# The first tile of chunk attention feeding a GELU MLP: reciprocals by fp32 transposes, an earlier half of w_in, and the last AV inside mm1

## The chip, the core and the metric

The kernel runs on one core of a Trainium2 chip. The metric is the device time of one execution in microseconds (us); the time before is the median of three runs. A profile of one execution gives a span, from its first to its last instruction, which is about 2 us shorter than the device time.

## What is computed

The reference does attention within chunks of 64 positions (batch 8, 8 heads, 576 positions, head size 64) and feeds the result, as 4608 tokens of 512 features, to a two-layer MLP with the exact GELU between the layers (512 to 2048 to 512). Everything comes in and goes out as float32.

```python
scores = scale * np.matmul(q_c, k_c.transpose(0, 1, 2, 4, 3))      # 9 chunks of 64 x 64 for each head
scores = scores - np.max(scores, axis=-1, keepdims=True)
attn = np.exp(scores)
attn = attn / (np.sum(attn, axis=-1, keepdims=True) + 1e-09)
out = np.matmul(attn, v_c)
x = np.ascontiguousarray(attn_out.transpose(0, 2, 1, 3)).reshape(B * S, H * D)
h = x @ w_in
g = 0.5 * h * (1.0 + erf(h * inv_sqrt2))
return (g @ w_out).astype(np.float32)
```

## The kernel before

**Tiles.** There are nine tiles of 512 tokens. Tiles 0 to 7 are the first eight chunks of one batch entry each; tile 8 gathers the ninth chunk of all eight entries. Heads go in pairs, so a tile has four groups g, each of 128 features (two heads of 64). Matmuls take bf16 operands, cast on the chip from float32 arrivals that lie in six stage buffers.

**Attention of tile 0.** For each group, `att_Tq` and `att_Tk` (L147 and L153) transpose q and k on TensorE and copy them out of PSUM; k goes in two halves into a block-diagonal tile `k_bd`. `att_S` (L187) makes the scores and their exponential `pT`. Then the sums of the exponentials are taken, inverted and spread over the partitions as `rc`. Groups 0 and 1 do that with `att_sum` (L197): a matmul with ones, a 32 x 32 transpose on VectorE, a reciprocal and another transpose. Groups 2 and 3 use `att_sum_pe` (L262): four matmuls of two columns, a reciprocal on VectorE, and, in its inner function `spread`, fp32 matmuls with an identity on TensorE (L276) and a copy on ScalarE. `att_av` (L284) multiplies with V on TensorE (L289) and then makes `x[:, g]` on VectorE as the product of that and `rc` (L296).

**The MLP of a tile** is `phase` (L387). Its first half, mm1, has 16 slots f; each is four matmuls (ks = 0 to 3, L328) that take the four groups of x in turn, then a Gelu on ScalarE (L331). `first` slots are done together, ks by ks, and `between` names functions that are called ahead of a given ks of these. Its second half, mm2 (L384 for tile 0, L344 otherwise), multiplies with w_out. `extra1` and `extra2` name attention work of the next tile that is called between the slots.

**Who sets the order.** Everything stands under a manual schedule: each engine has one queue, and its instructions stand in it in the order in which the Python code emits them. A call of `att_av` therefore places its matmuls in TensorE's queue and its multiply in VectorE's queue at that point of the program. The code emits, in this order: the loads of tile 0's q and k, of V, and of w_in's parts 0 to 2; the attention of tile 0, which ends with `A[3]()`; the load of w_in's part 3 and of w_out, with q and k of tile 1 between; all casts of w_in, of most of w_out and of tile 1's q, k and V, on VectorE, ScalarE and GpSimd (`DV`, `AC`, `PO`); then `phase(0, ...)`, with tile 1's attention inside its second half; then the other tiles. w_in comes in four parts of 512 columns, each cast in four pieces `win[c](i, engine)`; slot f needs piece f % 4 of part f // 4. All loads go through one queue of the sync engine. `keep_warm` issues matmuls that only keep TensorE busy.

Of the kernel before, what the change touches and what calls it, by code (L numbers as in the profile page):

```python
# [11 lines left out]
def kernel(  # L12
# [9 lines left out]
    nc = tc.nc  # L22
    P = 128
    f32 = mybir.dt.float32
# [3 lines left out]
    B, H, S, D = q.shape  # L28
    CH = 64
    NC = S // CH  # L30
    J = 4
    PC = CH // J
    G = H // 2
# [4 lines left out]
    MT = CT * CH  # L38
# [20 lines left out]
    ident_f = consts.tile([P, P], f32, name="ident_f")  # L59
# [9 lines left out]
    k_bds = [consts.tile([P, CT, P], bf16, name=f"k_bd{i}") for i in range(G)]  # L69
# [22 lines left out]
    ps_mm = ctx.enter_context(tc.tile_pool(name="ps_mm", bufs=3, space=bass.MemoryType.PSUM))  # L92
    ps_tp = ctx.enter_context(tc.tile_pool(name="ps_tp", bufs=2, space=bass.MemoryType.PSUM))
# [9 lines left out]
    def load_qk(t, nm, h0=0, h1=H):  # L103

        st = tiles[t]
        src = q if nm == "q" else k
        if nm + "f" not in st:
            st[nm + "f"] = stage_tile()[:].rearrange("p (h j d) -> p h j d", h=H, j=J)
            st[nm] = ld.tile([P, G, J, 2, D], bf16, tag=nm, name=f"{nm}_nat")
        raw = st[nm + "f"]  # L110
        if t < B:
            nc.sync.dma_start(raw[:, h0:h1], src[t, h0:h1, 0:MT, :].rearrange("h (p j) d -> p h j d", j=J))  # L112
        else:
            for b in range(B):
                nc.sync.dma_start(
                    raw[PC * b:PC * (b + 1), h0:h1],
                    src[b, h0:h1, MT:S, :].rearrange("h (p j) d -> p h j d", j=J))

    def load_v(t, gs=range(G)):
        if "vf" not in tiles[t]:  # L120
            tiles[t]["vf"] = stage_tile()[:].rearrange("p (g i d) -> p g i d", g=G, d=D)
        vf = tiles[t]["vf"]
        for g in gs:
            for r in range(2):
                if t < B:
                    src = v[t, 2 * g + r, 0:MT, :].rearrange("(i key) d -> key i d", key=CH)
                else:
                    src = v[:, 2 * g + r, MT:S, :].rearrange("b key d -> key b d")
                nc.sync.dma_start(vf[CH * r:CH * (r + 1), g], src)

    def cast_qk(t, nm, g, copy):
        st = tiles[t]
        copy(st[nm][:, g].rearrange("p j r d -> p r j d"), st[nm + "f"][:, 2 * g:2 * g + 2])  # L133

    def cast_v(t, r, copy, gs=slice(0, G)):
        sl = slice(CH * r, CH * (r + 1))
        copy(v_bds[t % NV][sl, :, gs, sl].rearrange("p i g d -> p g i d"), tiles[t]["vf"][sl, gs])  # L137
# [9 lines left out]
    def att_Tq(t, g, copy):  # L147
        tp = transposed(t, "q", g)
        qT = work.tile([P, CT, CH], bf16, tag="qT", name="qT", bufs=5)
        copy(qT[:].rearrange("p i (c j) -> p i c j", j=J), tp)  # L150
        tiles[t]["qT", g] = qT

    def att_Tk(t, g, copy):  # L153
        tp = transposed(t, "k", g)
        for r in range(2):
            sl = slice(CH * r, CH * (r + 1))
            copy(k_bds[g][sl, :, sl].rearrange("p i (c j) -> p i c j", j=J), tp[sl])  # L157


    def flip(t, nm):  # L160
# [101 lines left out]
    def att_sum_pe(t, g):  # L262

        pT = tiles[t]["pT", g]
        sT = ps_at.tile([P, MT // P, 2], f32, tag="at", name="sT")
        for m in range(MT // P):
            nc.tensor.matmul(sT[:, m], pT[:].rearrange("p i c -> p (i c)")[:, m * P:(m + 1) * P], ones_r[:],
                             start=True, stop=True)
        rr = work.tile([P, MT // P, 2], f32, tag="rr", name="rr", bufs=2)
        nc.vector.reciprocal(rr[:], sT[:])  # L270

        def spread():
            rc_ps = ps_mm.tile([P, MT], f32, tag="mm", name="rc_ps")
            for m in range(MT // P):
                for r in range(2):
                    nc.tensor.matmul(rc_ps[CH * r:CH * (r + 1), m * P:(m + 1) * P],  # L276
                                     rr[:, m, r:r + 1].to_broadcast([P, D]), ident_f[:],
                                     start=True, stop=True, tile_position=(0, CH * r))
            rc = work.tile([P, NB, 32], f32, tag="rc", name="rc", bufs=4)
            nc.scalar.copy(rc[:].rearrange("p n e -> p (n e)"), rc_ps[:])  # L280
            tiles[t]["rc", g] = rc
        return spread

# [14 lines left out]
    NB = MT // 32  # L298
    DV, AC, PO = nc.vector.tensor_copy, nc.scalar.copy, nc.gpsimd.tensor_copy

    def att_units(t, cq=DV, ck=DV):
        tiles[t]["x"] = xpool.tile([P, G, MT], bf16, tag="x", name="x")
        T = []
        for g in range(G):
            T += [lambda g=g: att_Tq(t, g, cq), lambda g=g: att_Tk(t, g, ck if t == 0 or g < 2 else DV)]
        S_ = [lambda g=g: att_S(t, g) for g in range(G)]
        if t > 1:
            T = [lambda g=g: flip_k(t, g, ck) for g in range(G)]
            S_ = [lambda g=g: (att_S_flipped(t, g), att_part(t, g)) for g in range(G)]
        if t > 0:  # L310
            U = [lambda g=g: att_total(t, g, g + 2) for g in (0, 2)] + [lambda g=g: att_rc(t, g) for g in range(G)]
        else:
            U = [lambda g=g: att_sum(t, g) for g in range(G)]
        A = [lambda g=g: att_av(t, g) for g in range(G)]
        return T, S_, U, A
# [71 lines left out]
    def phase(t, extra1, extra2, by_rows=False, between={}):  # L387
        nms = MT // P
        order = [(ms, qt) for ms in range(nms) for qt in range(NQ)]
        if by_rows:  # L390
            order = [(None, f) for f in range(FF - FC)] + [(ms, NQ - 1) for ms in range(nms)]
        first = 3 if t == 1 else 1
        mm1_slot(t, 0, first, between)
        for f in range(first, FF):
            for u in extra1.get(f, ()):
                u()
            mm1_slot(t, f)
        for s, (ms, qt) in enumerate(order):
            for u in extra2.get(s, ()):
                u()  # L400
            if ms is None:
                mm2_rows(t, qt)
            else:
                mm2_slot(t, ms, qt)
        for u in extra2.get("end", ()):
            u()
# [6 lines left out]
    NWC = 4  # L413
    WC = d_ff // NWC
    FC = FF // NWC

    def load_w_in(c, parts=1):
        raw = stage_tile()[:].rearrange("p (ks n) -> p ks n", ks=KS)
        n = WC // parts
        for a in range(parts):  # L420
            nc.sync.dma_start(raw[:, :, a * n:(a + 1) * n], w_in_v[:, :, c * WC + a * n:c * WC + (a + 1) * n])

        def cast(i, copy):
            copy(w_in_sb[:, :, c * WC + i * P:c * WC + (i + 1) * P], raw[:, :, i * P:(i + 1) * P])
        return cast
# [14 lines left out]
    def keep_warm(n):  # L440
        warm = ps_mm.tile([P, MT], f32, tag="mm", name="warm")
        for _ in range(n):
            nc.tensor.matmul(warm[:], rest[:, 0:P], rest[:], start=True, stop=True)
# [3 lines left out]
    def act_table(func):  # L447
        nc.scalar.activation(act_scratch[:], rest[:, 0:1], func)  # L448

    with tc.manual_schedule():  # L450
        for g in range(G):
            for nm in "qk":
                load_qk(0, nm, 2 * g, 2 * g + 2)
        load_v(0)
        win = [load_w_in(c, 2 if c < 2 else 1) for c in range(NWC - 1)]
        act_table(Act.Exp)
        keep_warm(7)
        zero_k(k_bds[0], nc.gpsimd)
# [6 lines left out]
        zero_k(k_bds[3], nc.gpsimd)  # L465
        cast_qk(0, "k", 2, PO)
        cast_qk(0, "k", 3, PO)
        for g in range(G):
            cast_v(0, 0, PO, slice(g, g + 1))
            cast_v(0, 1, PO, slice(g, g + 1))  # L470
        cast_qk(0, "q", 0, DV)
        T[0]()
        cast_qk(0, "q", 1, DV)
# [8 lines left out]
        keep_warm(1)  # L482
        S_[1]()
        cast_qk(0, "q", 3, DV)
        U[0]()
        T[5]()
        T[6]()
        T[7]()
        U[1]()
        S_[2]()  # L490
        keep_warm(1)
        S_[3]()
        keep_warm(1)
        p2 = att_sum_pe(0, 2)
        p3 = att_sum_pe(0, 3)
        A[0]()
        p2()
        A[1]()
        p3()
        A[2]()  # L500
        keep_warm(1)
        A[3]()
        win.append(load_w_in(NWC - 1))
        wout = [load_w_out(0)]
        for i, eng in enumerate((PO, AC, DV, PO)):
            win[0](i, eng)
        act_table(Act.Gelu)
        load_qk(1, "q")
        wout.append(load_w_out(1))
        for c in range(1, NWC):  # L510
# [23 lines left out]
        for g in range(G):  # L534
            for r in range(2):
                cast_v(1, r, PO, slice(g, g + 1))

        T, S_, U, A = att_units(1, AC, AC)
        def next_qk():
            for nm in "qk":  # L540
# [3 lines left out]
        def sums():  # L544
# [4 lines left out]
                      9: [T[7], S_[1], next_qk], 10: [S_[2], lambda: att_sum(1, 0), lambda: wout[3](2, DV)],  # L549
                      11: [lambda: wout[3](3, AC), S_[3]], 12: [sums],  # L550
                      13: [A[0], lambda: over[0](2), lambda: over[0](3), U[3]], 14: [A[1], U[4]], 15: [A[2], U[5]]},
              by_rows=True)
        last_av = {1: [A[3], lambda: rows_out(0, 3)]}
        pool_cast_qk(2)
        for t in range(1, NT):
# [47 lines left out]
```

The softmax here doesn't subtract the row's maximum and nothing guards it: scores larger than these inputs give would overflow.

## Time and profile before

| What | us |
|---|---|
| Device time, median of 3 (lowest and highest) | 291.13 (290.92 to 292.19) |
| Span of the profiled execution | 288.9 |
| TensorE busy in the span | 278.2 |
| VectorE busy | 154.8 |
| ScalarE busy | 170.1 |
| GpSimd busy | 98.8 |
| First matmul of mm1 of tile 0 starts | 17.40 |
| First matmul of mm2 of tile 0 starts | 31.72 |

The profile's busy shares are averages over the span. A timeline row gives start, length, engine, line, operation, operands and count, and in brackets how long the engine sat idle before it and what ended that. A window row gives its length, the busy time of each engine with the number of instructions in parentheses, the granted TensorE clock, the mean busy share of the 16 DMA engines, and what they moved. Ends of matmuls are modelled, so a single matmul looks longer than the step from one to the next.

### The profile page before, as it was taken

What the parts mean: (1) busy time and instruction counts of PE and PEld (TensorE: products, weight loads), DVE (VectorE), ACT (ScalarE), POOL (GpSimd) and SP (SyncE); (2) the same over time, 40 slices, a digit from 0 to 9 for tenths busy, and PEclk for the clock granted to TensorE, in tenths of its full rate; (3) what the DMA queues carried; (4) which work ended last, traced back from release to release, by engine and by line L of the source; (5) the groups of instructions that cost most, each with busy time, mean ns of one, the idle gap of its engine ahead of it and who ended that gap; (6) DMA issues with size and microseconds to landing.
All of it is one profiled execution on the core that took longest, in us unless ns stands there. A gap on an engine that the chain in (4) does not pass through costs nothing.

```text
span 288.9 us, 4859 instructions
## 1 busy us (share of the span) xinstructions
PE 278.2 (96%) x1836; PEld 138.5 (48%) x1870; DVE 154.8 (54%) x265; ACT 170.1 (59%) x329; POOL 98.8 (34%) x136
## 2 busy tenths in 40 slices
PE   7699999999999999999999999999999999999994
PEld 2454455445544554455445544554455445544444
DVE  6854349348805882749246935394268425850011
ACT  3767766967447844785468536763785368626400
POOL 6859758605651830262008400650003610000000
PEclk9999999999999999999999999999999999999999
DMA  6999999999799726961698259914999970120033
GB/s 222 247 360 404 393 337 265 254 207 286 191 291 311 168 99 161 325 145 74 161 261 234 76 138 285 233 73 115 163 130 131 265 147 2 39 106 2 0 73 73
DMA packets 96887, 53.79 MB, mean 186 GB/s; under 512 B 68576, under 2 KB 89312, under 8 KB 96864
## 3 DMA queue, kind: packets, MB, share of 16 engines
q1 hardware_dynamic: 96704, 53.36, 69.8%
q8 instruction: 14, 0.23, 0.3%
q10 hardware_dynamic: 160, 0.13, 0.2%
q14 instruction: 9, 0.07, 0.1%
HBM read 36.70 MB, written 9.44 MB: 160 GB/s over the span
## 4 chain that ended last, share of the span: by engine, by line
PE 90%; DVE 3%; ACT 3%; DMA 2%; issue 1%; SPq 0%; POOL 0%; DVEq 0%; POOLq 0%
PE h_ps L328 42%; PE y_ps L344 37%; PE av_ps L289 3%; PE y_ps L384 3%; PE s_ps L180 2%; DMA arrival<-in_k_dram 2%; ACT k_bd L157 2%; PE y_ps L369 1%; DVE x L296 1%; PE tp L144 1%; PE rc_ps L276 1%; DVE rc L259 1%; ACT pT L194 1%; SPq L112 0%; PE s_ps L192 0%
## 5 line engine op out<-in xcount | busy, mean ns | idle before, releaser
L328 PE MATMUL h_ps<-x,w_in_sb 128*128 128x512 bf16 x565 | 125.8, 379 | 1.0 <-DVE x L296 0.4
L331 ACT ACTIVATE h<-h_ps 128x512 bf16<-128x512 f32 x144 | 85.5, 597 | 62.5 <-PE h_ps L328 62.4
L344 PE MATMUL y_ps<-w_out_sb,h 128*128 128x512 bf16 x493 | 117.9, 379 | 0.9
L328 PEld LDWEIGHTS <-w_in_sb 128*128 128x128 bf16 x576 | 56.2, 98 | 68.4 <-issue 1.2
L344 PEld LDWEIGHTS <-h 128*128 128x128 bf16 x512 | 46.0, 98 | 46.5 <-issue 0.2
L172 DVE COPY k_bd<-k_t 64x512 bf16<-64x512 bf16 x56 | 35.6, 636 | 53.6 <-DMA k_t<-k_nat 52.6
L133 POOL CAST q_nat<-arrival 128x512 bf16<-128x512 f32 x31 | 21.2, 720 | 95.0 <-DMA arrival<-in_q_dram 95.0
L137 POOL CAST v_bd<-arrival 64x512 bf16<-64x512 f32 (+1 forms) x30 | 36.3, 1210 | 20.5 <-DMA arrival<-in_v_dram 13.3
L296 DVE TENSOR_TENSOR x<-av_ps,rc 128x512 bf16<-128x512 f32 x36 | 24.8, 692 | 4.7 <-PE av_ps L289 1.4
L133 POOL CAST k_nat<-arrival 128x512 bf16<-128x512 f32 x34 | 20.1, 625 | 11.2 <-DMA arrival<-in_k_dram 9.2
L448 ACT ACT_TABLE_LOAD x18 | 23.1, 1283 | 1.0 <-PEq L587 0.7
L353 DVE COPY y_sb<-y_ps 128x512 f32<-128x512 f32 x11 | 7.6, 691 | 29.7 <-PE y_ps L344 27.8
L353 ACT COPY y_sb<-y_ps 128x512 f32<-128x512 f32 x24 | 13.8, 580 | 14.7 <-PE y_ps L344 14.4
L239 DVE STREAM_TRANSPOSE pt<-pT 128x256 f32<-128x256 f32 x28 | 12.2, 437 | 18.8 <-ACT pT L183 18.8
L259 DVE STREAM_TRANSPOSE rc<-rb 128x512 f32<-128x512 f32 x31 | 21.5, 692 | 0.2 <-ACT rb L229 0.2
L242 DVE TENSOR_REDUCE part<-pt 128x16 f32<-128x512 bf16 x28 | 19.2, 686 | 1.0
L250 ACT COPY other<-part 32x32 f32<-32x32 f32 x56 | 12.0, 215 | 10.4 <-DVE part L242 9.9
L289 PEld LDWEIGHTS <-v_bd 128*128 128x128 bf16 x288 | 13.0, 98 | 8.0 <-issue 0.3
L183 ACT ACTIVATE pT<-s_ps 128x512 bf16<-128x512 f32 x28 | 14.7, 590 | 0.0
L289 PE MATMUL av_ps<-pT,v_bd 128*128 128x64 bf16 x288 | 14.3, 193 | 0.2
L180 PEld LDWEIGHTS <-k_bd 128*128 128x128 bf16 x224 | 10.4, 98 | 6.6
L384 PE MATMUL y_ps<-w_out_sb,h 128*128 128x512 bf16 x46 | 11.9, 379 | 0.4 <-ACT h L331 0.3
(68 smaller groups left out, 136.5 us busy)
## 6 DMA issues: line engine op xcount, KB each, us to landing
arrival<-in_v_dram SPq DMA_DIRECT2D x72, 128.0 KB, 4.1
out_dram<-y_sb SPq DMA_DIRECT2D x32, 256.0 KB, 2.3
arrival<-in_q_dram SPq DMA_DIRECT2D x7, 1024.0 KB, 6.7
arrival<-in_k_dram SPq DMA_DIRECT2D x7, 1024.0 KB, 9.1
arrival<-in_moe_w_out_dram SPq DMA_DIRECT2D x4, 1024.0 KB, 12.2
arrival<-in_moe_w_in_dram SPq DMA_DIRECT2D x4, 512.0 KB, 6.2
arrival<-in_moe_w_in_dram SPq DMA_DIRECT2D x2, 1024.0 KB, 10.4
arrival<-in_q_dram SPq DMA_DIRECT2D x4, 256.0 KB, 4.7
```

Source lines behind the costliest of these rows:

```text
L133: copy(st[nm][:, g].rearrange("p j r d -> p r j d"), st[nm + "f"][:, 2 * g:2 * g + 2])
L137: copy(v_bds[t % NV][sl, :, gs, sl].rearrange("p i g d -> p g i d"), tiles[t]["vf"][sl, gs])
L172: copy(k_bds[g][sl, :, sl].rearrange("p i (c j) -> p i c j", j=J), src[sl])
L259: nc.vector.transpose(rc[:], src.to_broadcast([P, NB, 32]))
L289: nc.tensor.matmul(av_ps[:, i, :], v_bds[t % NV][:, i, g, :], st["pT", g][:, i, :], start=True, stop=True)
L296: nc.vector.tensor_tensor(x, av, rc, op=mybir.AluOpType.mult)
L328: nc.tensor.matmul(h_ps[a][:], w_in_sb[:, ks, (f + a) * P:(f + a + 1) * P], st["x"][:, ks, :], start=(ks == 0), stop=(ks == KS - 1))
L331: nc.scalar.activation(st["h"][:, f + a, :], h_ps[a][:], Act.Gelu)
L344: nc.tensor.matmul(y_ps[:], st["h"][:, f, ms * P:(ms + 1) * P], w_out_sb[:, f, :], start=(f == 0), stop=(f == FF - 1))
L353: (AC if ms < 3 and t + 1 < NT else DV)(y_sb[:], y_ps[:])
L384: nc.tensor.matmul(tiles[t]["y_ps", ms][:], tiles[t]["h"][:, f, ms * P:(ms + 1) * P], w_out_sb[:, f, :], start=(f == 0), stop=False)
L448: nc.scalar.activation(act_scratch[:], rest[:, 0:1], func)
```

## The change

It is for the start of the kernel, up to the first tile's mm1. It has these parts.

- All four groups of tile 0 use `att_sum_pe`. Its spread is made of fp32 transposes on TensorE in place of fp32 matmuls: for each 128 columns a transpose of 128 rows and then one of 64, which overwrites the upper head's values in the lower half. Groups 2 and 3 take their PSUM from the transposes' pool.
- For groups 2 and 3 of tile 0 one half of the `k_bd` copy goes to VectorE.
- The first half of w_in's part 0 is loaded ahead of the last pair of V. Its pieces 0, 1 and 2 are cast on VectorE, piece 3 on GpSimd; the second cast of V's last pair goes to VectorE.
- The last AV of tile 0, `A[3]`, is no longer called at the end of the attention but, as `A0[3]`, ahead of ks = 1 inside mm1 of tile 0. Two slots of that mm1 are done together (`first` is 2).
- Two warm-up matmuls go.

```diff
-    def att_Tk(t, g, copy):
+    def att_Tk(t, g, copies):
...
-            copy(k_bds[g][sl, :, sl].rearrange("p i (c j) -> p i c j", j=J), tp[sl])
+            copies[r](k_bds[g][sl, :, sl].rearrange("p i (c j) -> p i c j", j=J), tp[sl])
...
         def spread():
-            rc_ps = ps_mm.tile([P, MT], f32, tag="mm", name="rc_ps")
+            pool, tag = (ps_mm, "mm") if g < 2 else (ps_tp, "tp")
+            rc_ps = pool.tile([P, NB, 32], f32, tag=tag, name="rc_ps")
+            flat = rc_ps[:].rearrange("p n e -> p (n e)")
             for m in range(MT // P):
-                for r in range(2):
-                    nc.tensor.matmul(rc_ps[CH * r:CH * (r + 1), m * P:(m + 1) * P],
-                                     rr[:, m, r:r + 1].to_broadcast([P, D]), ident_f[:],
-                                     start=True, stop=True, tile_position=(0, CH * r))
+                for r in (1, 0):
+                    nc.tensor.transpose(flat[0:CH * (r + 1), m * P:(m + 1) * P],
+                                        rr[:, m, r:r + 1].to_broadcast([P, CH * (r + 1)]), ident_f[:])
...
-        first = 3 if t == 1 else 1
+        first = (2, 3, 1)[min(t, 2)]
         mm1_slot(t, 0, first, between)
...
-        load_v(0)
-        win = [load_w_in(c, 2 if c < 2 else 1) for c in range(NWC - 1)]
+        load_v(0, range(G - 1))
+        win = [load_w_in(0, 2, lambda: load_v(0, [G - 1]))]
+        win += [load_w_in(c, 2 if c < 2 else 1) for c in range(1, NWC - 1)]
...
         S_[1]()
         cast_qk(0, "q", 3, DV)
-        U[0]()
+        p0 = att_sum_pe(0, 0)
         T[5]()
+        p0()
         T[6]()
         T[7]()
-        U[1]()
+        p1 = att_sum_pe(0, 1)
         S_[2]()
+        p1()
         keep_warm(1)
         S_[3]()
-        keep_warm(1)
         p2 = att_sum_pe(0, 2)
+        p2()
+        A[0]()
+        A[1]()
         p3 = att_sum_pe(0, 3)
-        A[0]()
-        p2()
-        A[1]()
         p3()
+        win[0](0, DV)
         A[2]()
-        keep_warm(1)
-        A[3]()
+        win[0](1, DV)
+        cast_v(0, 1, DV, slice(G - 1, G))
         win.append(load_w_in(NWC - 1))
         wout = [load_w_out(0)]
-        for i, eng in enumerate((PO, AC, DV, PO)):
-            win[0](i, eng)
         act_table(Act.Gelu)
+        for i in (2, 3):
+            win[0](i, (DV, PO)[i % 2])
         load_qk(1, "q")
...
+        A0 = A
         T, S_, U, A = att_units(1, AC, AC)
...
-              by_rows=True)
+              by_rows=True, between={1: [A0[3]]})
```

More of the change, by code (lines that the diff above doesn't have):

```diff
@@ L272, in spread @@
         def spread():
-            rc_ps = ps_mm.tile([P, MT], f32, tag="mm", name="rc_ps")
+            pool, tag = (ps_mm, "mm") if g < 2 else (ps_tp, "tp")
+            rc_ps = pool.tile([P, NB, 32], f32, tag=tag, name="rc_ps")
+            flat = rc_ps[:].rearrange("p n e -> p (n e)")
             for m in range(MT // P):
-                for r in range(2):
-                    nc.tensor.matmul(rc_ps[CH * r:CH * (r + 1), m * P:(m + 1) * P],
-                                     rr[:, m, r:r + 1].to_broadcast([P, D]), ident_f[:],
-                                     start=True, stop=True, tile_position=(0, CH * r))
+                for r in (1, 0):
+                    nc.tensor.transpose(flat[0:CH * (r + 1), m * P:(m + 1) * P],
+                                        rr[:, m, r:r + 1].to_broadcast([P, CH * (r + 1)]), ident_f[:])
             rc = work.tile([P, NB, 32], f32, tag="rc", name="rc", bufs=4)
-            nc.scalar.copy(rc[:].rearrange("p n e -> p (n e)"), rc_ps[:])
+            nc.scalar.copy(rc[:], rc_ps[:])
             tiles[t]["rc", g] = rc
@@ L304, in att_units @@
         for g in range(G):
-            T += [lambda g=g: att_Tq(t, g, cq), lambda g=g: att_Tk(t, g, ck if t == 0 or g < 2 else DV)]
+            T += [lambda g=g: att_Tq(t, g, cq), lambda g=g: att_Tk(t, g, (AC, DV) if t == 0 and g > 1 else [AC if t == 0 or g < 2 else DV] * 2)]
         S_ = [lambda g=g: att_S(t, g) for g in range(G)]
@@ L415, with load_w_in @@
     FC = FF // NWC
-    def load_w_in(c, parts=1):
+    def load_w_in(c, parts=1, between=lambda: None):
         raw = stage_tile()[:].rearrange("p (ks n) -> p ks n", ks=KS)
@@ L420, in load_w_in @@
         for a in range(parts):
+            if a == 1:
+                between()
             nc.sync.dma_start(raw[:, :, a * n:(a + 1) * n], w_in_v[:, :, c * WC + a * n:c * WC + (a + 1) * n])
@@ L467 @@
         cast_qk(0, "k", 3, PO)
-        for g in range(G):
+        for g in range(G - 1):
             cast_v(0, 0, PO, slice(g, g + 1))
             cast_v(0, 1, PO, slice(g, g + 1))
+        cast_v(0, 0, PO, slice(G - 1, G))
         cast_qk(0, "q", 0, DV)
```

## The prediction

> **What bounds the kernel now.** I read the busy shares first, then the windows by stage, then the timelines of TensorE and VectorE around the start of mm1, and last the timeline of GpSimd. The page says that TensorE is nearly always busy:
>
> ```profile
> PE 278.2 (96%) x1836; PEld 138.5 (48%) x1870; DVE 154.8 (54%) x265; ACT 170.1 (59%) x329; POOL 98.8 (34%) x136
> ```
>
> The windows by stage (length, then busy us and instructions of PE, PEld, DVE, ACT, POOL, then clock, DMA share, GB/s) put most of its idle time ahead of the first mm1 and show saturated DMA engines during it:
>
> ```profile
> 0.00:17.38 17.38, 12.89 (x151) 7.54 (x154) 12.28 (x25) 9.43 (x17) 13.32 (x34) 1.00 0.87 250
> 18.56:31.72 13.16, 13.11 (x60) 5.96 (x61) 5.86 (x10) 9.62 (x17) 10.20 (x12) 1.00 1.06 399
> 37.06:39.00 1.94, 1.94 (x10) 0.88 (x9) 1.18 (x2) 0.47 (x1) 1.62 (x2) 1.00 1.05 409
> ```
>
> From 18.56 us on TensorE runs almost without a gap, so the time is the moment at which mm1 of the first tile can run freely, plus a fixed amount of matmul work. In the timeline of TensorE (start, length, line, operation, count) that moment is the fourth matmul, which waits for the last quarter of x; the three before it began at 17.40:
>
> ```profile
> 17.40 0.94 PE L328 MATMUL h_ps<-x,w_in_sb 128*128 128x512 bf16 x3
> 18.56 5.77 PE L328 MATMUL h_ps<-x,w_in_sb 128*128 128x512 bf16 x26 [0.22 <-DVE x L296]
> ```
>
> 26 matmuls in 5.77 us, each shown 0.379 long, are (5.77 - 0.38) / 25 = 0.216 us apart. The timeline of VectorE shows what stands in its queue behind the last multiply (L296): casts, each held by a transfer.
>
> ```profile
> 17.22 1.29 DVE L296 TENSOR_TENSOR x<-av_ps,rc 128x512 bf16<-128x512 f32 x2 [0.74 <-PE av_ps L289]
> 18.42 0.70 DVE L424 CAST w_in_sb<-arrival 128x512 bf16<-128x512 f32 x1
> ...
> 26.30 1.99 DVE L424 CAST w_in_sb<-arrival 128x512 bf16<-128x512 f32 x2 [1.37 <-DMA arrival<-in_moe_w_in_dram]
> 28.91 1.18 DVE L432 CAST w_out_sb<-arrival 128x512 bf16<-128x512 f32 x2 [0.62 <-DMA arrival<-in_moe_w_out_dram]
> 31.62 0.43 DVE L133 CAST q_nat<-arrival 128x512 bf16<-128x512 f32 x1 [1.53 <-DMA arrival<-in_q_dram]
> 34.15 1.18 DVE L432 CAST w_out_sb<-arrival 128x512 bf16<-128x512 f32 x2 [2.10 <-DMA arrival<-in_moe_w_out_dram]
> 37.06 1.18 DVE L133 CAST k_nat<-arrival 128x512 bf16<-128x512 f32 x2 [1.73 <-DMA arrival<-in_k_dram]
> ```
>
> The casts follow the arrivals of one MiB each, 2.6 us apart: 1.05 MB in 2.6 us is 403 GB/s, what the windows show. So their times are set by bytes, not by the engine.
>
> **What the Trainium skill says.** "TensorE: Matmul & The Clock Gate", Part 1 (engine queue depths), calls the ACT and DVE queues strict FIFO and GpSimd's too; TensorE only pulls weight loads ahead, its matmuls stay in order. The trace agrees for GpSimd, whose memset of v_bds[1] (L520) needs no transfer and yet stands idle behind a cast that waits for one:
>
> ```profile
> 21.27 0.87 POOL L424 CAST w_in_sb<-arrival 128x512 bf16<-128x512 f32 x1 [0.34 <-DMA arrival<-in_moe_w_in_dram]
> 22.09 1.79 POOL L520 MEMSET v_bd<- 64x2048 bf16 x1
> ```
>
> The same page, Part 1 (the HAM clock gate), says that after an idle window of about 3.4 us the array runs at half rate until it has been busy for about as long. The trace agrees at the start of the kernel: seven warm-up matmuls take 3.17 us, and three later ones 0.81 us.
>
> ```profile
> 1.20 3.17 PE L443 MATMUL warm<-rest 128*128 128x512 bf16 x7 [1.20 <-DVE rest L47]
> 5.33 0.81 PE L443 MATMUL warm<-rest 128*128 128x512 bf16 x3
> ```
>
> The later three are (0.81 - 0.38) / 2 = 0.215 us apart, the first seven 0.43 (their weight loads start at 1.60, 2.02, 2.45, 2.88 and 3.31). The clock column reads 1.00 in both stretches, so it does not show this gate.
>
> **The change, part by part.** The step that decides is the last one: AV of group 3 is now called from inside mm1. The matmuls of A0[3] go where they are wanted, between the first and second ks of slots 0 and 1. But A0[3] also emits the multiply that makes x[:,3], and it does so when phase(0) is written out, after every cast of the section in between has been emitted on VectorE. In the built program VectorE's queue holds, after the multiply of group 2: two casts of w_in's first part around it, one of V, one more of that part, two each for w_in parts 1, 2 and 3, two of w_out part 0, one of q of tile 1, two of w_out part 1, two of k of tile 1, and only then the multiply of group 3, as its 41st instruction. The ks=3 matmul of slot 0 waits for exactly that instruction (VectorE's semaphore at 41). Behind that matmul stands everything else of TensorE, and behind TensorE the Gelus.
>
> 1. The new wait. The two k casts began at 37.06 and took 1.18: they end at 38.24. The multiply is 0.69 (L296), so x[:,3] is there at 38.24 + 0.03 + 0.69 = 38.96, and TensorE starts 0.04 later (18.52 to 18.56 before): 39.00. Before it was 18.56. Shift: 20.44 us.
> 2. What is done before the wait. Slots 0 and 1 run together (`first` is 2), so ks 0 to 2 of slot 1 are already computed: 3 x 0.216 = 0.65 us less to do. AV's matmuls also lie before it.
> 3. The cold array. TensorE idles from about 21 to 39 us, far more than 3.4 us. Nothing of the kernel before shows such a restart in mid-kernel. Bounds: 0, or half of the 4.1 us between the first warm-up matmul (1.20) and the first group seen at full rate (5.33), which is 2.1. From the page's 3.4 us the loss is half of it, and I take 1.7 as an estimate.
> 4. Do the loads get later? k's load was issued at 23.97 and landed at 37.06: some 13 us in the queue, behind 1 MiB every 2.6 us. The loads ahead of it wait for stage buffers, which the casts of V and of w_in parts 0 and 1 free. If the prologue makes these casts 2 us later, the queue still holds several us of work. The order and bytes from w_in part 2 on are unchanged. Cost 0, with 1 us either way for the range.
> 5. The other edits, at nothing, all hidden by the wait that ends at 39.00. (a) Two att_sum go from VectorE: 2 x (0.72 + 0.25 + 0.71) = 3.4 us, and their two matmuls; in come two column sums (4 matmuls of 2 columns, 0.25 a group), two reciprocals (0.19) and two copies on ScalarE (0.58 each). (b) All four spreads use fp32 transposes, 8 a group in place of the 16 passes that take 1.02 on the chain of waits. No row shows one; one pass of 128 columns as in tp is 0.055 us, so between 8 x 0.055 = 0.44 and the 1.02 of today, I take 0.6. (c) One half of two k_bd copies moves from ScalarE to VectorE, 2 x 0.58. (d) Half of w_in's first part, 0.5 MiB, goes ahead of the last V pair: 1.3 us earlier for the one, as much later for the pair. (e) Casts of that part move to VectorE. (f) Warm-up matmuls go. I put the arrival at the blocked matmul at 20 to 22 us by following the queues; whatever it is, 17 us of slack cover it.
>
> Nothing gives the time back: TensorE is busy in 13.11 of 13.16 us, then in 18.05 of 18.63, and I cannot name a later wait above 0.3 us that an earlier arrival would spare. Sum: 20.44 - 0.65 + 1.7 = 21.5; with the median of 291.13 this is 312.6 us.
>
> **The rivals.**
> - Queue held, array not cold: 291.13 + 20.44 - 0.65 = 310.9. For it: the clock column never falls. Against: the seven slow matmuls at the start. 0.08.
> - Queue held, loads or re-warming later: stage buffers freed late by the VectorE casts push k's arrival out by 1.5 us or more, or the array needs another 3.4 us: about 314.3. For it: the loads wait on those buffers. Against: the 13 us of queue. 0.10.
> - Queue held, arrival of k 1 us earlier (transfers do better while TensorE stands still): 311.6. Against: the DMA engines already show a share of 1.06. It lies in the main case's range, and I count it there.
> - The multiply is not held, as if it stood right behind group 2's in the queue. Then the prologue counts: VectorE has 3.4 us less of transposes and 0.65 us of slot 1 fills the wait, against 1.2 us of new k_bd halves and casts in front of x. That is some 0.7 us gained: 290.4, a little faster. Limits are w_in parts 1 and 2, whose casts were 0.5 to 0.9 us ahead of their slots. For it: nothing in the trace of before, which has no such multiply out of place; it would need a queue that lets a ready instruction pass. Against: the memset above and the semaphore value. 0.03, with 0.01 for a result within 0.5%.
>
> **How the numbers follow.** The main case has 0.78 and gives 312.6. The range of 310.2 to 314.6 takes in the rival without a cold array and most of the late one. Chances: faster 0.02, same 0.02, slower 0.96.
>
> **What the trace after would show.** Right: TensorE idle for some 17 us up to about 39 us with VectorE's x as what ended it; the multiply of group 3 directly after k's two casts; matmuls 0.43 us apart for 3 to 4 us after it; the spreads near 0.6 us; the rest of the run as long as before. Wrong: x of group 3 made before w_in part 1 is cast, k's casts far from 37 us, or no slow matmuls after the gap.

## The result and the profile after

The changed kernel takes 313.31 us (median; 312.17 to 314.6) against 291.02 (290.74 to 292.19): a ratio of 1.0759, with a 95% interval of 1.0708 to 1.081. It is slower by about 22 us, as forecast (312.6).

The page of the kernel after shows that TensorE has 5.3 us more busy time, but 17 us more idle time:

```profile
span 311.4 us, 4901 instructions
PE 283.5 (91%) x1874; PEld 141.0 (45%) x1874; DVE 153.5 (49%) x266; ACT 169.5 (54%) x328; POOL 97.3 (31%) x134
```

Its windows, cut at the idle time and at the restart behind it (columns as in the windows of before):

```profile
21.00:38.90 17.90, 1.65 (x13) 0.75 (x14) 9.54 (x16) 1.02 (x2) 14.08 (x16) 0.66 1.06 402
38.90:43.00 4.10, 3.00 (x8) 1.08 (x8) 1.04 (x2) 1.33 (x3) 3.10 (x6) 0.50 1.11 355
```

In the first window TensorE works for 1.65 of 17.9 us while the DMA engines stay saturated; in the second it runs eight matmuls in 4.1 us. The timeline of TensorE gives the two ends of the idle time and what ended it, and that of VectorE what stood in front of the multiply:

```profile
22.45 1.03 PE L331 MATMUL h_ps<-x,w_in_sb 128*128 128x512 bf16 x4
39.99 6.33 PE L331 MATMUL h_ps<-x,w_in_sb 128*128 128x512 bf16 x20 [16.52 <-DVE x L299]
```

```profile
35.45 1.18 DVE L437 CAST w_out_sb<-arrival 128x512 bf16<-128x512 f32 x2 [2.10 <-DMA arrival<-in_moe_w_out_dram]
38.17 1.18 DVE L133 CAST k_nat<-arrival 128x512 bf16<-128x512 f32 x2 [1.54 <-DMA arrival<-in_k_dram]
39.27 0.68 DVE L299 TENSOR_TENSOR x<-av_ps,rc 128x512 bf16<-128x512 f32 x1
```

The four matmuls at 22.45 are ks 1 and 2 of slots 0 and 1; the AV of group 3 was done just before them. Its multiply starts 16.7 us later, as soon as k of tile 1 has been cast, although all that it needs was ready. The weight loads that follow the wait show the cold array, nine steps of 0.43 us and then the full rate:

```profile
40.00 0.10 PEld L331 LDWEIGHTS <-w_in_sb 128*128 128x128 bf16 x1 [16.80 <-issue]
40.38 0.15 PEld L331 LDWEIGHTS <-w_in_sb 128*128 128x128 bf16 x1 [0.28 <-issue]
...
43.36 0.15 PEld L331 LDWEIGHTS <-w_in_sb 128*128 128x128 bf16 x1 [0.27 <-issue]
43.79 10.24 PEld L331 LDWEIGHTS <-w_in_sb 128*128 128x128 bf16 x48 [0.27 <-issue]
```

The span grew by 311.4 - 288.9 = 22.5 us. The terms from the two traces: the fourth matmul of slot 0 moved from 18.56 to 39.99, 21.43; slot 1 is three matmuls ahead, -0.65; nine slow steps cost 9 x (0.43 - 0.216) = 1.9. Together 22.7, which leaves -0.2 for all the rest of the run.

### The profile page after: what moved, and what is told of

Read it like the earlier page. It is cut to its first block, busy times and chain, and to the rows that moved or that the text cites. A ratio compares the mean times of both kernels' runs of the same rounds, so it can differ in the third digit from the quotient of the medians.

```text
span 311.4 us, 4901 instructions
## 1 busy us (share of the span) xinstructions
PE 283.5 (91%) x1874; PEld 141.0 (45%) x1874; DVE 153.5 (49%) x266; ACT 169.5 (54%) x328; POOL 97.3 (31%) x134
## 4 chain that ended last, share of the span: by engine, by line
PE 83%; DMA 8%; SPq 3%; DVE 2%; POOL 1%; ACT 1%; issue 1%; DVEq 0%
PE h_ps L331 40%; PE y_ps L347 34%; DMA arrival<-in_k_dram 4%; PE y_ps L387 3%; DMA arrival<-in_moe_w_in_dram 2%; PE av_ps L292 2%; PE s_ps L180 2%; SPq L129 2%; DMA arrival<-in_q_dram 2%; PE y_ps L372 1%; DVE x L299 1%; DVE rc L259 1%; POOL v_bd L529 1%; SPq L426 1%; PE tp L144 1%
## 5 line engine op out<-in xcount | busy, mean ns | idle before, releaser
L331 PE MATMUL h_ps<-x,w_in_sb 128*128 128x512 bf16 x576 | 128.5, 383 | 17.6 <-DVE x L299 16.5
L347 PE MATMUL y_ps<-w_out_sb,h 128*128 128x512 bf16 x512 | 120.5, 379 | 0.0
L137 POOL CAST v_bd<-arrival 64x512 bf16<-64x512 f32 (+1 forms) x29 | 35.6, 1228 | 40.7 <-DMA arrival<-in_v_dram 36.4
L239 DVE STREAM_TRANSPOSE pt<-pT 128x256 f32<-128x256 f32 x28 | 12.2, 437 | 23.3 <-ACT pT L183 23.3
L157 DVE COPY k_bd<-tp 64x512 bf16<-64x512 bf16 x6 | 4.1, 690 | 24.8 <-PE tp L144 23.8
```

Source lines behind the costliest of these rows:

```text
L331: nc.tensor.matmul(h_ps[a][:], w_in_sb[:, ks, (f + a) * P:(f + a + 1) * P], st["x"][:, ks, :], start=(ks == 0), stop=(ks == KS - 1))
L347: nc.tensor.matmul(y_ps[:], st["h"][:, f, ms * P:(ms + 1) * P], w_out_sb[:, f, :], start=(f == 0), stop=(f == FF - 1))
```

## The experiments

The theory is that the multiply of group 3 is held in VectorE's queue by the casts emitted ahead of it, and that the array is cold when it is let through. Its rivals are an AV inside mm1 as such, the reordered loads, and the rebuilt prologue.

**The slots emitted early.**

```diff
         cast_v(0, 1, DV, slice(G - 1, G))
+        act_table(Act.Gelu)
+        mm1_slot(0, 0, 2, {1: [A[3]]})
         win.append(load_w_in(NWC - 1))
...
-        mm1_slot(t, 0, first, between)
+        if t > 0:
+            mm1_slot(t, 0, first, between)
...
-              by_rows=True, between={1: [A0[3]]})
+              by_rows=True)
```

> The changed kernel, but slots 0 and 1 of the first mm1, with the last AV inside them, are emitted directly after the second cast of V's last pair, so that the multiply of group 3 stands ahead of all later casts in VectorE's queue. Nothing else is changed. Theory (the multiply is held by the casts in front of it): the wait of 16.5 us and the cold restart go; TensorE is let through at about 23 us in place of 40, since that multiply still follows the cast of V at 22.1, and the time is 291.0 + (22.9 - 18.6) - 0.65 = about 294.7 us. Rival (an AV inside mm1 itself, or the order of the loads, costs the time): still 310 us or more.

Measured: 294.84 us (before 291.11; ratio 1.0135, 1.0119 to 1.015). In its timeline of VectorE the multiply of group 3 now waits for nothing but its AV:

```profile
21.94 0.69 DVE L299 TENSOR_TENSOR x<-av_ps,rc 128x512 bf16<-128x512 f32 x1 [0.65 <-PE av_ps L292]
```

The long wait is gone with the same AV inside the same mm1, only emitted ahead of the later casts. So neither an AV inside mm1 as such nor the new order of the loads makes the 22 us. The rest of the change is no gain either: 3.7 us slower than before, hidden in the changed kernel by the long wait. The expected 294.7 is met in part by chance, since the trace also has a wait of 1.07 us at slot 2, treated below, that the expectation does not count.

**The last part alone, on the kernel before.**

```diff
-        A[3]()
...
+        A0 = A
         T, S_, U, A = att_units(1, AC, AC)
...
-              by_rows=True)
+              by_rows=True, between={1: [A0[3]]})
```

> The kernel before, with one edit: the last AV of tile 0 is called ahead of ks = 1 of slot 0 inside the first mm1, as in the changed kernel; one slot at a time. Theory (held multiply): the multiply comes after k's two casts, which end at 38.2 to 39.3, so mm1 waits until 39 to 40; 291.0 + 20.4 to 21.4 + 1.9 for the restart = 313.3 to 314.3 us. Rival (transposes, loads, casts of the prologue cost the time): within 1 us of 291.

Measured: 314.03 us (ratio 1.0768, 1.0726 to 1.0811). The one edit brings the whole loss. Its timeline of TensorE:

```profile
39.28 5.91 PE L328 MATMUL h_ps<-x,w_in_sb 128*128 128x512 bf16 x14 [21.05 <-DVE x L296]
```

Here the restart was longer: weight loads 0.43 us apart until 44.78, 13 steps, 2.8 us lost. The span, 312.3, is 23.4 above that of before; 39.28 - 18.56 + 2.8 = 23.5.

**A smaller dose of the same wait.** The slots are emitted behind the casts of w_in and ahead of those of w_out:

```diff
                 nc.gpsimd.memset(v_bds[1][r, :, :, o], 0.0)
+        mm1_slot(0, 0, 2, {1: [A[3]]})
         for i in range(FC):
             wout[0](i, DV if i % 2 == 0 else PO)
```

> The changed kernel, but slots 0 and 1 of the first mm1 with the last AV are emitted behind the casts of w_in and ahead of those of w_out and of tile 1's q and k: a smaller dose of the same wait. Theory: VectorE's last w_in cast ends at 28.3 to 29.7, the multiply 0.7 later, TensorE is let through at 29.1 to 30.5, idle for some 6 us, so the restart is cold as before: 291.0 + 10.5 to 11.9 - 0.65 + 1.9 = 302.8 to 304.2 us. Rival (not the place in VectorE's queue): as the changed kernel, 313.

Measured: 303.48 us (ratio 1.043, 1.0413 to 1.0448). The multiply started at 29.26, right after the last w_in cast, and TensorE was let through at

```profile
29.99 14.53 PE L331 MATMUL h_ps<-x,w_in_sb 128*128 128x512 bf16 x57 [7.54 <-DVE x L299]
```

So the time follows the place in VectorE's queue: 294.8, 303.5 and 313.3 us for a multiply ahead of the later casts, behind those of w_in, and behind those of k.

**Kept warm.** 72 warm-up matmuls stand ahead of the ks = 3 matmuls that wait:

```diff
-by_rows=True, between={1: [A0[3]]})
+by_rows=True, between={1: [A0[3]], 3: [lambda: keep_warm(72)]})
```

> The changed kernel with 72 warm-up matmuls (15.6 us at 0.216 each) ahead of the ks = 3 matmuls that wait, so that TensorE is busy for nearly all of the wait. Theory (half rate after the idle time): the nine matmuls at 0.43 us apart after the wait become 0.216 apart, and the time falls by 9 x 0.21 = 1.9 us to about 311.4. Rival (the slow matmuls come from something else that happens then, such as casts and loads): they stay 0.43 apart and the time stays at 313.3.

Measured: 312.16 us (310.81 to 313.08). The medians differ by 1.2 us, with ranges that overlap, so the trace has to decide. In its timeline of TensorE the wait ends at the same time as in the changed kernel, and in its windows the clock stays at 1.00:

```profile
36.75 1.24 PE L448 MATMUL warm<-rest 128*128 128x512 bf16 x5
39.96 6.20 PE L331 MATMUL h_ps<-x,w_in_sb 128*128 128x512 bf16 x27 [1.97 <-DVE x L299]
```

```profile
38.90:43.00 4.10, 3.04 (x15) 1.38 (x15) 1.01 (x2) 2.27 (x4) 3.10 (x6) 1.00 1.08 323
```

27 matmuls in 6.20 us are (6.20 - 0.38) / 26 = 0.224 apart, where the changed kernel has 20 in 6.33. The casts of that stretch are the same and the loads nearly so (DMA share 1.08 against 1.11), so the slow steps come from TensorE's own idle time, as the Trainium skill says ("TensorE: Matmul & The Clock Gate", Part 1, the HAM clock gate). The span of the profiled execution is 309.5, shorter by 1.9: nine steps of 0.21. The granted clock of the four executions goes with their times. Two were at 0.999 and 1.00 over the whole execution and took 311.31 and 310.81 us; two were at 0.995 and 0.993 and took 313.08 and 313.01. So the latter still had a stretch at a lower clock somewhere; no trace shows where. The changed kernel reads 0.966 to 0.971 in all four.

**Where the other 3.7 us are.** The waits of TensorE in the early-slots kernel (who waited for whom, us in total, times, longest) have two entries on VectorE that the waits of the kernel before lack:

```profile
PE rc_ps L280 <- DVE rr L270: 2.8, 3, 1.3
PE h_ps L331 <- DVE w_in_sb L430: 2.3, 2, 1.2
```

First the transposes alone, on the kernel before: only the body of `spread`, its PSUM pool included, is that of the changed kernel.

```diff
-                for r in range(2):
-                    nc.tensor.matmul(rc_ps[CH * r:CH * (r + 1), m * P:(m + 1) * P], ...
+                for r in (1, 0):
+                    nc.tensor.transpose(flat[0:CH * (r + 1), m * P:(m + 1) * P], ...
```

> The kernel before, with only the spreads of groups 2 and 3 made of fp32 transposes. The prediction took 0.6 us for such a spread against 1.02 of the fp32 matmuls; two lie on the path: 290.3 us. What the changed kernel's trace suggests is no gain, 8 transposes in 1.09 us: 291.1 us, with the first free matmul of mm1 within 0.2 us of 18.6.

Measured: 290.92 us against 291.03 (ratio 0.9997, 0.9983 to 1.0012). No difference. Here is one spread and the AV behind it, first in the kernel before and then in this one:

```profile
14.32 1.09 PE L276 MATMUL rc_ps<-ident_f,rr 128*64 128x128 f32 x16
15.34 0.41 PE L289 MATMUL av_ps<-pT,v_bd 128*128 128x64 bf16 x8
```

```profile
14.75 1.07 PE L278 MATMUL rc_ps<-ident_f,rr 128*128 128x128 f32 x8
15.65 0.40 PE L290 MATMUL av_ps<-pT,v_bd 128*128 128x64 bf16 x8
```

From the start of the spread to the AV behind it are 0.90 us; before it was 1.02. The Trainium skill calls the transpose mode four times faster for fp32 ("TensorE: Matmul & The Clock Gate", Terms, at xbus), without saying than what; nothing near that shows here. Each instruction is indeed one pass where the fp32 matmul takes two, but a pass takes twice as long: 8 are 0.11 us apart, (1.07 - 0.27) / 7, and the 16 passes of the narrower pairs 0.055.

Then the order on VectorE. The change also moved the AVs of groups 0 and 1 ahead of the column sums of group 3 (its diff shows it, its list of parts does not). Here, in the kernel with the early slots, the column sums and reciprocal of group 3 go ahead of these two AVs again:

```diff
         p2()
+        p3 = att_sum_pe(0, 3)
         A[0]()
         A[1]()
-        p3 = att_sum_pe(0, 3)
```

> The kernel with the early slots, with the column sums and the reciprocal of group 3 emitted ahead of the AVs of groups 0 and 1. Theory: its reciprocal no longer waits behind two multiplies in VectorE's queue (1.3 us), the wait of 1.2 us ahead of the fourth spread falls away, and everything behind it comes about 1 us earlier: 293.8 us. Rival (the casts alone set the time): 294.8 us.

Measured: 293.9 us (ratio 1.0088, 1.0062 to 1.0114), 0.9 less than with the early slots, or 1.4 by the ratios. In this kernel's waits the entry falls from 2.8 to 1.6, and the fourth spread follows the AVs without a gap.

The casts of w_in's first two pieces and of V put back on GpSimd and ScalarE:

```diff
+        cast_v(0, 1, PO, slice(G - 1, G))
...
-        win[0](0, DV)
+        win[0](0, PO)
         A[2]()
-        win[0](1, DV)
-        cast_v(0, 1, DV, slice(G - 1, G))
+        win[0](1, AC)
```

> The kernel with the early slots (294.84 us), with the casts of w_in's first two pieces and of V's last pair put back on GpSimd and ScalarE, where the kernel before has them. Theory (VectorE, in order, became the bottleneck of the prologue: the two w_in casts and the V cast, 0.4 + 0.4 + 0.7 us, stand in front of the multiply of group 3): that multiply starts about 1 us earlier than 21.9, and the third w_in cast is ready some 2 us earlier, so 292.8 us. Rival (the later V pair, or the spreads, cost the 3.7 us): within 0.5 us of 294.8.

Measured: 294.72 us (293.76 to 295.81; ratio 1.0131, 1.0088 to 1.0174). A miss: no gain can be told. The multiply came only 0.6 us earlier (21.37), since slot 1 now waited for ScalarE's cast, which stood behind the late copy of `rc`.

> Both edits: the casts back on their engines and the reciprocal of group 3 first. Theory: the gains nearly add, about 291.8 us, so that the other parts of the change together are worth nothing against the kernel before (291.1). If it is below 290.5, the remaining parts of the change are a gain.

With both edits: 292.46 us (ratio 1.0054, 1.0034 to 1.0074). With the reciprocal first the casts give 1.4 us, or 1.0 by the ratios, whose intervals overlap; alone they gave 0.1. The trace fits that: the copy of `rc` that held ScalarE's cast starts at 17.93 here and at 19.48 with the casts alone. So the gains do not add, the second opens only after the first, but with 4, 6 and 11 executions their sizes are rough. Against the kernel before 1.4 us remain, twice what was expected.

**What is left.** To that kernel the sums of groups 0 and 1 are put back (`U[0]()` and `U[1]()` in place of `p0` and `p1`, both `k_bd` halves on ScalarE):

> The kernel with both edits (292.46 us), and groups 0 and 1 back on the matmul with ones and VectorE's transposes, with their k_bd copies on ScalarE alone. Theory (the reciprocal of group 1 waits in VectorE's queue behind two k_bd halves and a copy of q, 1.3 us, and that sets the start of the remaining prologue): the loss of 1.4 us against the kernel before goes, 291.0 us. Rival (the later last pair of V and the early half of w_in cost it): 292.4 us.

Measured: 292.5 us (ratio 1.003, 1.0014 to 1.0045), so 1.3 us above before by the medians and 0.9 by the ratio. The rival was right in its number. In the profiled execution another cost had come in, which its window and its timeline of TensorE show:

```profile
13.50:16.00 2.50, 1.93 (x14) 1.65 (x12) 0.57 (x2) 0.24 (x1) 1.50 (x3) 0.62 1.00 278
```

```profile
14.13 1.97 PE L280 MATMUL rc_ps<-ident_f,rr 128*128 128x128 f32 x8 [0.57 <-DVE rr L270]
```

The array had fallen to half rate in the prologue, and a spread took 1.97 us. Not every execution seems to have this: the clock over the whole execution is 0.994 or less in 9 of the 22, the profiled one among them (median 292.7 us), and 0.998 or more in the other 13 (median 291.65). The change drops two warm-up matmuls, and without them TensorE may have had too little to do here. With three of them around the column sums of group 2:

```diff
         S_[3]()
+        keep_warm(1)
         p2 = att_sum_pe(0, 2)
+        keep_warm(2)
         p2()
```

> The kernel with the sums of groups 0 and 1 put back (292.5 us), with three warm-up matmuls around the column sums of group 2, one of which the kernel before also has there. In the run without them the array fell to half rate in the prologue (clock 0.62 from 13.5 to 18 us, the two spreads 1.97 and 1.38 us long in place of 1.09). Theory (the missing warm-up matmuls cost that, and the rest of the loss is gone): spreads of 1.09 us, 1.2 us less, 291.3 us. Rival (the later last pair of V, the wait for w_in's second piece and the queue of ScalarE hold the prologue anyway): 292.0 us or more.

Measured: 292.12 us (ratio 1.0024, 1.0009 to 1.0039), so the rival's number again. The spreads of the profiled execution were 1.09 and 1.07 us long, and 2 of the 14 executions read 0.994 or less. That the warm-up matmuls did this is likely but not certain, since the array also stayed at full rate in most executions without them. The time they should have saved is not seen, and the trace shows another wait, in this kernel's timelines of GpSimd and TensorE:

```profile
17.64 1.28 POOL L137 CAST v_bd<-arrival 64x512 bf16<-64x512 f32 x2 [1.95 <-DMA arrival<-in_v_dram]
18.98 1.17 POOL L430 CAST w_in_sb<-arrival 128x512 bf16<-128x512 f32 x2
```

```profile
19.64 0.39 PE L331 MATMUL h_ps<-x,w_in_sb 128*128 128x512 bf16 x1 [2.17 <-POOL w_in_sb L430]
```

GpSimd stands for 1.95 us at the last pair of V, which the change loads behind half of w_in, and the w_in casts that TensorE needs stand behind that cast. So the earlier half of w_in had arrived and could not be used. How much of the remaining 0.7 us this load order is stays open: it was not tried alone, and the pair of V was cast at 17.64 in this trace but at 16.54 in that of the kernel with both edits, which has the same load order.

**A cast held by a memset.** In the early-slots kernel TensorE waited 1.07 us at slot 2 for the third piece of w_in. Its timelines of VectorE, GpSimd and TensorE:

```profile
22.55 7.12 DVE L430 CAST w_in_sb<-arrival 128x512 bf16<-128x512 f32 x7
```

```profile
22.21 1.80 POOL L531 MEMSET v_bd<- 64x2048 bf16 x1
```

```profile
24.35 12.26 PE L331 MATMUL h_ps<-x,w_in_sb 128*128 128x512 bf16 x55 [1.07 <-DVE w_in_sb L430]
```

The first of these seven casts took 1.746 us, and ended 0.3 us after the memset; the one at 20.12 in the same trace took 0.42. The Trainium skill ("SBUF — State Buffer", Who interferes with whom) says that a VectorE copy or cast in a two-port mode and GpSimd share a pair of ports, and that whoever issues first has them for the whole instruction. The trace fits that, since the memset began 0.3 us ahead of the cast. As a test both memsets went behind the casts of w_out part 0:

```diff
-            if c < 3:
-                ...
-                nc.gpsimd.memset(v_bds[1][r, :, :, o], 0.0)
...
+        for c in (1, 2):
+            ...
+            nc.gpsimd.memset(v_bds[1][r, :, :, o], 0.0)
         load_v(1)
```

> The kernel with the early slots (294.84 us), with GpSimd's two memsets of v_bds[1] moved from between its w_in casts to behind its casts of w_out part 0. In the early-slots run the third piece of w_in, which TensorE waits for, took VectorE 1.75 us in place of 0.43, ending 0.3 us after the first of these memsets (22.21 to 24.01). Theory (the cast is held by the memset, over the port that the two engines share): the cast takes 0.43 to 0.9 us, TensorE's wait of 1.07 us ahead of slot 2 goes, 293.8 us. Rival (the cast is slow for another reason, or the gain is lost to the next wait): 294.8 us.

Measured: 294.65 us (ratio 1.0106, 1.0089 to 1.0123). The three casts, the awaited one first, took 0.42 us each and TensorE ran on into slot 2 without a gap, so the memset was what held the cast. That it did so through the ports is the skill's account, which no run here separates from another:

```profile
23.46 1.09 DVE L430 CAST w_in_sb<-arrival 128x512 bf16<-128x512 f32 x3
```

The gain in time is 0.2 us by the medians and 0.8 by the ratios, whose intervals overlap a little, so it is not shown. The two traces cannot be set side by side as they are: this prologue ran 0.8 us later (the fourth spread at 18.91 in place of 18.09), and that lateness is there from the second q of tile 0 on (cast at 7.08 in place of 6.20), ahead of anything that was edited.

**The idea at its right place.** On the kernel before, slots 0 and 1 are done together and emitted directly behind the last AV, with w_in's first two pieces both cast on GpSimd:

```diff
-        for i, eng in enumerate((PO, AC, DV, PO)):
-            win[0](i, eng)
-        act_table(Act.Gelu)
+        win[0](0, PO)
+        win[0](1, PO)
+        act_table(Act.Gelu)
+        mm1_slot(0, 0, 2)
+        win[0](2, DV)
+        win[0](3, PO)
```

> The kernel before, with the idea of the last part of the change done at the right place: slots 0 and 1 of the first mm1 together, emitted directly after the last AV and the casts of w_in's first two pieces (both on GpSimd), ahead of all other casts. The AV itself stays ahead of mm1. Theory: the multiply of group 3 ends at 18.5 as before; the three matmuls of slot 1 that need only groups 0 to 2 are done in the wait, 3 x 0.216 = 0.65 us, of which some 0.2 us pushes the next one back: 290.6 us, at the edge of what can be told from 291.0. Rival (w_in's arrival sets the pace of mm1 anyway): 291.0.

Measured: 290.96 us against 291.24 (ratio 0.999, 0.9976 to 1.0005). No difference can be told. The timeline of TensorE shows where a gain ends:

```profile
17.44 3.78 PE L328 MATMUL h_ps<-x,w_in_sb 128*128 128x512 bf16 x16
21.42 10.69 PE L328 MATMUL h_ps<-x,w_in_sb 128*128 128x512 bf16 x47 [0.20 <-DVE w_in_sb L425]
```

The first four slots run without a gap, but slot 4 then waits for the arrival of w_in part 1. It begins at 21.42; in the kernel before at 18.56 + 13 x 0.216 = 21.37. In this trace that part was cast at 20.94, in that of before at 20.03, so whether the arrival is the limit in the other executions too is not shown. No version beat the kernel before by more than can be measured.

## Why the prediction was right

The time, 313.31 against 312.6, and its cause were right, and it owes little to errors that cancel: the forecast was 1.0 us short in the first step and 0.2 in the third, and 0.2 too long in the rest. By its steps:

1. **The new wait.** The mechanism was right to the instruction: the multiply follows k's casts (timeline), the one edit alone brings the loss, and moving the place in the queue moves the time. The size was 1 us short: TensorE went on at 39.99, not 39.00, because k was cast at 38.17, not 37.06.
2. **Work done before the wait**, 0.65 us: right.
3. **The cold array**: 1.9 us measured (nine slow steps) against 1.7, and the warm run takes just that away. On the kernel before with the late AV it was 2.8, above the stated bound of 2.1: a restart has no fixed length in these traces. The remark that the clock column does not show this gate was wrong: it reads 0.66 and 0.50 here. It is right for the start of the kernel before, where the column reads 1.00 over seven slow matmuls.
4. **Later loads**, put at 0 with 1 us either way: the stream was up to 1.1 us later. k was cast at 37.27, 37.45, 37.93, 38.14 and 38.17 in the early-slots, late-AV, w_in-dose, warm and changed kernels, against 37.06 before. Much of that is likely scatter between executions, and not the change. Three kernels have the loads in the order of before and cast k at 37.45 (late AV), 37.74 (transposes alone) and 37.86 (paired slots); 37.06 is the earliest of all the traces. The second q of tile 0, loaded ahead of all that was changed, was cast between 5.76 and 7.08 in them. What makes this scatter stays open.
5. **The other edits, hidden**: right for the total, since the terms above leave -0.2 us. Two sizes in it were wrong. A spread holds the chain for 0.9 us (1.09 as shown), not 0.6. And the blocked matmul was reached at about 23.3 us (22.45 + 4 x 0.216), not 20 to 22.

The rival without the wait was mis-sized, and on the wrong side: it said 290.4, "a little faster", but with the slots emitted early the kernel took 294.84. What failed is the sum that counted VectorE's 3.4 us of saved transposes as a gain; nor do its terms, 3.4 + 0.65 - 1.2 = 2.85, give the 0.7 that it states. With the transposes put back the time did not rise (292.46 and 292.5 us; 1.0054 and 1.003 of the kernel before). The sum left out that the remaining small work stands in one queue in a worse order (the reciprocal of group 3 behind two multiplies, w_in and V casts ahead of the last multiply) and, as far as one trace shows, that the last pair of V came later.

## What to carry to other kernels

Where each engine has one queue in program order, moving a call moves all the instructions it emits, on every engine: an AV placed well on TensorE can leave its multiply behind a dozen casts on VectorE. Before moving a call, list for each engine what now stands ahead of its instructions, and at which arrivals that is held. If matmuls are to fill a wait, emit them earlier, next to the work that they wait for, and do not move that work to where they stand. Count an idle TensorE of 7 us or more (the shortest such wait here was 7.5) as a restart of 2 to 3 us on top.

## What the runs showed of the hardware that was not expected

- A VectorE cast of 128x512 took 1.746 us beside a GpSimd memset of 1.80 us, and 0.42 us when that memset was moved behind it.
- Eight fp32 transposes of 128 and 64 columns (1.07 us as shown) take nearly the time of 16 narrow fp32 passes (1.09).
- The restart at half rate lasted 9 steps in two profiles (waits of 16.5 and 7.5 us) and 13 in another (21 us), and in one trace the array fell to half rate in a prologue that was merely thin (clock 0.62 from 13.5 to 16 us, where no idle time of TensorE after its first matmul was above 0.8 us).
- A load with nothing changed ahead of it was cast up to 1.3 us apart in the traces (the second q of tile 0, at 5.76 to 7.08 us).
